# A memory-attention and squared-ReLU MLP kernel: all steps up to the last weight conversion issued in the order of a list schedule, batch 0 for 8 units, batch 1 for 16, then batch 0

## The chip, the cores and the metric

The kernel runs on one core of one Trainium2 chip. Its engines work side by side, each through its own queue in order: TensorE (PE, with PEld for weight loads), VectorE (DVE), ScalarE (ACT), GpSimd (POOL) and SyncE (SP), which issues the transfers. They wait for one another by semaphores. The metric is the device time of one execution in microseconds.

## The reference

Eight batches, 8 heads, 512 tokens of 64 numbers and 32 state rows per head. Tokens attend to the states and states to the tokens; the 544 rows per batch, 4,608 rows of 512 in all, go through an MLP with 2,048 hidden columns and a squared ReLU.

```python
scores = scale * np.matmul(x, state.transpose(0, 1, 3, 2))
a = softmax(scores)                      # over the 32 states
xread = np.matmul(a, state)
a2 = softmax(scale * np.matmul(state, x.transpose(0, 1, 3, 2)))   # over the 512 tokens
sread = np.matmul(a2, x)
x = concatenate([xread, sread])          # per batch, heads side by side
r = np.maximum(x @ w_in, 0.0)
return ((r * r) @ w_out).astype(np.float32)
```

The weights come as 64-bit floats, the inputs as 32-bit ones.

## The kernel before, in words

For tokens, x @ w_in is not formed from xread. Per batch the kernel computes z = state @ w_in (tile pz, line 151, then z_hi and z_lo) and multiplies it by the transposed attention a (a_hi, a_lo): ph = a z, line 314. Every 32-bit operand of the two big products is split into a rounded part hi (a cast by ScalarE, line 80) and a rest lo (a subtraction by VectorE, line 83), and hi·hi, lo·hi and hi·lo are added up.

The work is cut into units, one per batch and per f chunk of 128 hidden columns, 16 per batch. A unit has an up part, six products into ph (L314), relu on ScalarE (L316), a square (L318 on ScalarE for the first 16 units, L320 on VectorE after that), the split into g_hi and g_lo, and a down part two units later, twelve products into the four accumulators po (L340). z is made in pieces of one, two or four f chunks; z tiles of four chunks have two buffers, ph and g two, the raw weight tile three (RAW), the float tile wof one.

Before batch b's first unit its attention must stand: scores in pst (L196), a copy for the states' softmax (e, L208), a transposing move into q (L236), maximum, difference, exponential, sum, reciprocal and product (L243 to L252; L245 on ScalarE), a transposing move back into at (L255) and the split. Batch 0 does that in two halves, the others in one piece.

A weight pair covers two f chunks and 1 MB. wi_raw and wo_raw hold 64-bit words; a conversion is a scaling on ScalarE (L102) and a shift and two joins on VectorE (L105, L111, L115). w_in then lies in wi; w_out is made in wof and split into wo_hi and wo_lo. There are eight pairs of each.

Units come in the order of BOTH (line 61): batch 0 up to f chunk 4, batch 1 up to 8, batch 0 the rest, batch 1 the rest, then batches 2 to 7 and a last part for the states' rows. Each stretch ends with four moves or additions from po into sum. The first four units and what they need are written out by hand in begin (line 513), in a fixed order for VectorE, SyncE and ScalarE; keep holds back the lo subtraction of a step and issues it later. After that mlp (line 301) goes unit by unit, and aux issues, at two slots per unit, the conversions that are due (spread evenly by weights, line 575), z pieces and the later batches' attention; up to the end of batch 0 VectorE and SyncE keep the order of issue, with lo parts one slot late, while a scheduler places TensorE and ScalarE.

Of the kernel before, what the change touches and what calls it, by code (L numbers as in the profile page):

```python
# [9 lines left out]
F32 = mybir.dt.float32  # L10
# [8 lines left out]
def memory_attention_then_relu2_ffn(  # L19
# [41 lines left out]
    BOTH = ((0, 4), (1, 8), (0, NFC), (1, NFC))  # L61
    LATE = 2

# [4 lines left out]
    ps_x = ctx.enter_context(tc.tile_pool(name="ps_x", bufs=1, space=bass.MemoryType.PSUM))  # L68

# [7 lines left out]
    held = []  # L77

    def split(hi, lo, src, eng_lo):
        nc.scalar.copy(out=hi, in_=src)  # L80

        def rest():
            eng_lo.tensor_sub(out=lo, in0=src, in1=hi.bitcast(F32))  # L83

        held[-1].append(rest) if held else rest()

    def keep(step):

        held.append([])
        emit(step)  # L90
        parts_ = held.pop()
        return lambda: [f() for f in parts_]

    def singles(out_f, words):
# [7 lines left out]
        nc.scalar.activation(out_f, high.bitcast(F32), AF.Abs, scale=2.0**-112)  # L102
# [7 lines left out]
        def join():  # L110
# [3 lines left out]
            )  # L114
            mark[:] = [nc.vector.scalar_tensor_tensor(  # L115
# [4 lines left out]
        return shift, join  # L120
# [5 lines left out]
    def z_piece(b, units, first):  # L126

        def run():
            with tc.high_priority(offset=HURRY):
                make()  # L130

        def make():
# [23 lines left out]
            if not first:  # L156
                split(z_hi[:, :, dst], z_lo[:, :, dst], both[:, :, :width], nc.vector)
                return
            for g in range(NG):
                split(z_hi[:, g, dst], z_lo[:, g, dst], pz[g], nc.vector)  # L160
        return run
# [3 lines left out]
    def attention(b):  # L165
# [13 lines left out]
        def fetch_t():  # L179
            my["t"] = sb.tile([P, HG, S], F32, name="xt_raw", bufs=1)  # L180
# [10 lines left out]
        def scores():  # L191
# [16 lines left out]
            nc.scalar.copy(out=my["e2"], in_=pst)  # L208
# [17 lines left out]
        def soft(gs):  # L226
# [14 lines left out]
            def soft1():  # L241
                q1 = flat(my["q1"])
                nc.vector.tensor_reduce(out=flat(my["m1"])[:, :, 0], in_=q1, axis=AX.X, op=ALU.max)  # L243
                nc.vector.tensor_sub(out=q1, in0=q1, in1=wide(my["m1"]))
                nc.scalar.activation(q1, q1, AF.Exp, scale=SCALE)  # L245

            def soft1b():
                q1, s1 = flat(my["q1"]), flat(my["s1"])
                nc.vector.tensor_reduce(out=s1[:, :, 0], in_=q1, axis=AX.X, op=ALU.add)
                nc.vector.tensor_scalar_add(s1, s1, EPS)  # L250
                nc.vector.reciprocal(s1, s1)
# [49 lines left out]
    def mlp(parts, begin, aux):  # L301
# [45 lines left out]
        for n in range(begin(up, down), len(todo_) + 2):  # L347
# [8 lines left out]
            if n >= 2:  # L356
                down(n - 2)
# [361 lines left out]
```

## Time and profile before

| | us |
|---|---|
| median of 3 runs | 701.27 (701.07 to 701.54) |
| profiled execution | 701.49 |
| its span | 699.7 |
| PE busy | 660.0 |
| DVE busy | 374.5 |
| ACT busy | 290.4 |

The span runs from the first to the last instruction of the profiled execution. Of the chain that ended last, PE has 89%. The mean granted TensorE clock is 0.987. Busy time of PE has modelled ends, so a row of several products shows more than their start-to-start pace.

### The profile page before, as it was taken

What the parts mean: (1) busy time and instruction counts of PE and PEld (TensorE: products, weight loads), DVE (VectorE), ACT (ScalarE), POOL (GpSimd) and SP (SyncE); (2) the same over time, 40 slices, a digit from 0 to 9 for tenths busy, and PEclk for the clock granted to TensorE, in tenths of its full rate; (3) what the DMA queues carried; (4) which work ended last, traced back from release to release, by engine and by line L of the source; (5) the groups of instructions that cost most, each with busy time, mean ns of one, the idle gap of its engine ahead of it and who ended that gap; (6) DMA issues with size and microseconds to landing.
All of it is one profiled execution on the core that took longest, in us unless ns stands there. A gap on an engine that the chain in (4) does not pass through costs nothing.

```text
span 699.7 us, 9593 instructions
## 1 busy us (share of the span) xinstructions
PE 660.0 (94%) x3896; PEld 496.6 (71%) x3896; DVE 374.5 (54%) x528; ACT 290.4 (41%) x470; POOL 24.4 (3%) x44
## 2 busy tenths in 40 slices
PE   1675999999999999999999999999999999999996
PEld 0343777778777777678777776777768767788895
DVE  4868778864847534643356333743474334343553
ACT  3445576452534333433344233433343233333442
POOL 0000000000010100010001000100002000000000
PEclk9898899999999999999999999999999999999999
DMA  8333335203113001300040003100111001000101
GB/s 311 120 121 120 121 125 200 101 5 120 63 61 121 5 0 56 127 5 1 0 181 5 1 0 126 56 1 1 59 64 59 3 1 60 1 1 0 61 1 30
DMA packets 15803, 43.59 MB, mean 62 GB/s; under 512 B 1296, under 2 KB 3344, under 8 KB 13840
## 3 DMA queue, kind: packets, MB, share of 16 engines
q1 hardware_dynamic: 15568, 42.73, 17.1%
q8 instruction: 30, 0.49, 0.3%
q10 hardware_dynamic: 192, 0.26, 0.2%
q14 instruction: 13, 0.11, 0.0%
HBM read 34.08 MB, written 8.91 MB: 61 GB/s over the span
## 4 chain that ended last, share of the span: by engine, by line
PE 89%; DVE 2%; ACT 2%; issue 1%; DMA 1%; SPq 0%
PE po L340 53%; PE ph L314 28%; PE pz L151 4%; PE pst L196 1%; PE pr L279 1%; PE pt L267 1%; DMA wi_raw<-w_in 1%; DVE wof L115 0%; DVE wof L111 0%; ACT g_hi L80 0%; ACT wo_hi L80 0%; ACT z_hi L80 0%; ACT ph L318 0%; DVE wo_lo L83 0%; DVE wi L111 0%
## 5 line engine op out<-in xcount | busy, mean ns | idle before, releaser
L340 PE MATMUL po<-wo_hi,g_hi 128*128 128x512 f32 x544 | 216.9, 401 | 9.6 <-ACT wo_hi L80 4.9
L340 PE MATMUL po<-wo_lo,g_hi 128*128 128x512 f32 x544 | 214.7, 397 | 1.3 <-DVE wo_lo L83 1.2
L320 DVE TENSOR_TENSOR ph<-ph,r 128x512 f32<-128x512 f32 (+1 forms) x128 | 84.9, 663 | 134.2 <-ACT r L316 134.0
L316 ACT ACTIVATE r<-ph 128x512 f32<-128x512 f32 (+1 forms) x144 | 82.9, 575 | 177.5 <-PE ph L314 177.4
L340 PE MATMUL po<-wo_hi,g_lo 128*128 128x512 f32 x544 | 156.4, 394 | 0.0
L83 DVE TENSOR_TENSOR g_lo<-ph,g_hi 128x512 fp32r<-128x512 f32 (+1 forms) x144 | 94.7, 659 | 91.1 <-ACT g_hi L80 70.4
L340 PEld LDWEIGHTS po<-wo_hi,g_hi 128*128 128x128 f32 x544 | 103.0, 190 | 42.3 <-ACT g_hi L80 8.7
L80 ACT CAST g_hi<-ph 128x512 fp32r<-128x512 f32 (+1 forms) x144 | 81.1, 563 | 117.2 <-DVE ph L320 75.0
L340 PEld LDWEIGHTS po<-wo_lo,g_hi 128*128 128x128 f32 x544 | 103.0, 190 | 30.0 <-issue 6.7
L340 PEld LDWEIGHTS po<-wo_hi,g_lo 128*128 128x128 f32 x544 | 101.8, 189 | 22.4 <-issue 0.8
L314 PE MATMUL ph<-a_hi,z_hi 128*128 128x512 f32 x256 | 84.3, 412 | 7.9 <-ACT a_hi L80 5.8
L314 PE MATMUL ph<-a_hi,z_lo 128*128 128x512 f32 x256 | 82.8, 402 | 0.0
L314 PE MATMUL ph<-a_lo,z_hi 128*128 128x512 f32 x256 | 80.3, 396 | 0.0
L314 PEld LDWEIGHTS ph<-a_hi,z_hi 128*128 128x128 f32 x256 | 46.9, 192 | 32.6 <-ACT a_hi L80 8.2
L83 DVE TENSOR_TENSOR z_lo<-pz,z_hi 128x1024 fp32r<-128x1024 f32 (+2 forms) x39 | 40.0, 1029 | 41.6 <-ACT z_hi L80 41.5
L314 PEld LDWEIGHTS ph<-a_hi,z_lo 128*128 128x128 f32 x256 | 49.0, 192 | 16.1 <-issue 5.4
L314 PEld LDWEIGHTS ph<-a_lo,z_hi 128*128 128x128 f32 x256 | 48.4, 190 | 11.7 <-DVE wof L105 0.8
L80 ACT CAST z_hi<-pz 128x1024 fp32r<-128x1024 f32 (+2 forms) x39 | 33.3, 859 | 50.1 <-PE ph L314 26.7
L151 PE MATMUL pz<-wi,sp_raw 64*32 64x512 f32 (+2 forms) x592 | 36.9, 557 | 7.3 <-DVE wi L115 6.9
L290 POOL COPY sr<-rd 32x128 f32<-32x128 f32 x32 | 9.2, 288 | 393.0 <-DVE rd L284 391.9
L151 PEld LDWEIGHTS pz<-wi,sp_raw 64*32 64x32 f32 x592 | 6.8, 107 | 22.6 <-DVE wi L115 9.3
L196 PE MATMUL pst<-xt_raw,sp_raw 64*32 64x512 f32 x128 | 14.6, 714 | 8.1 <-DMA xt_raw<-xT 6.8
(61 smaller groups left out, 387.6 us busy)
## 6 DMA issues: line engine op xcount, KB each, us to landing
xt_raw<-xT SPq DMA_DIRECT2D x8, 1024.0 KB, 4.9
wo_raw<-w_out SPq DMA_DIRECT2D x8, 1024.0 KB, 4.9
xn_raw<-xn SPq DMA_DIRECT2D x8, 1024.0 KB, 5.7
out<-sum SPq DMA_DIRECT2D x32, 256.0 KB, 3.8
wi_raw<-w_in SPq DMA_DIRECT2D x7, 1024.0 KB, 4.8
wi_raw<-w_in SPq DMA_DIRECT2D x2, 512.0 KB, 6.9
sp_raw<-stP SPq DMA_DIRECT2D x8, 64.0 KB, 1.9
out<-os__5381 SPq DMA_DIRECT2D x2, 64.0 KB, 1.7
```

What stands on the lines that cost most here:

```text
L80: nc.scalar.copy(out=hi, in_=src)
L83: eng_lo.tensor_sub(out=lo, in0=src, in1=hi.bitcast(F32))
L151: nc.tensor.matmul(pz[g][j * N:(j + 1) * N], lhsT=state[b][rows, j, :], rhs=wi[rows, j, cols], start=True, stop=True,)
L196: nc.tensor.matmul(pst[j * N:(j + 1) * N, g, :], lhsT=state[b][rows, j, :], rhs=my["t"][rows, j, :], start=True, stop=True,)
L267: nc.tensor.transpose(out=pt[:, g, t, :], in_=my["e2"][:, g, t * P:(t + 1) * P], identity=ident)
L279: nc.tensor.matmul(pr[j * N:(j + 1) * N, g, :D], lhsT=my["e"][:, g, t, j * N:(j + 1) * N], rhs=my["n"][:, t, h * D:(h + 1) * D], start=t = ...
L290: nc.gpsimd.tensor_copy(out=sr[b // GB][at:at + N, j * NG * D:(j + 1) * NG * D], in_=rd[j * N:(j + 1) * N].rearrange("p g d -> p (g d)"),)
L314: nc.tensor.matmul(ph, lhsT=w, rhs=v, start=m == 0, stop=m == len(todo) - 1)
L316: nc.scalar.activation(r, ph, AF.Relu)
L320: nc.vector.tensor_mul(out=ph, in0=ph, in1=r)
L340: nc.tensor.matmul(po[t], lhsT=g, rhs=w, start=i == 0 and j == 0, stop=i == last and j == 2)
```

## The change

The hand-written begin and the spread of conversions give way to one plan over the first 24 units, those of the first two stretches, and everything they need. BOTH becomes batch 0 up to f chunk 8, batch 1 up to 16, batch 0 the rest; so there are three stretches in place of four. The helpers return their steps apart (parts_of gives the cast and the subtraction, singles gives scaling, shift and two joins, up gives five steps, the attention ten). Each step goes into Plan with an engine, an assumed duration, and the names of the steps it needs; buffers that must be free are written as needs too. run takes, again and again, the engine that can start first, and of its steps that can start within 0.35 of then the one with the longest chain behind it, and issues it; the assumed times only set the order. All four engines keep that order. Further: the copy of the scores (keep) comes after the transposing move, xT of batch 1 goes into the xn_raw buffer and is loaded before the first w_out, z pieces after the first stretch are always four chunks wide, and the loop after the plan places no conversions.

```diff
-    BOTH = ((0, 4), (1, 8), (0, NFC), (1, NFC))
+    BOTH = ((0, 8), (1, NFC), (0, NFC))
     LATE = 2
+    TURN = 4
...
+    class Plan:
+        def __init__(self):
+            self.steps, self.order = {}, []
+        def add(self, name, engine, cost, run, needs=(), more=0.0, line=None):
+            assert name not in self.steps
+            self.steps[name] = engine, cost, cost + more, run, set(needs) | {line} - {None}, line
+        def run(self):
+            users = {n: [] for n in self.steps}
+            for n, (*_, needs, _) in self.steps.items():
+                for m in needs:
+                    users[m].append(n)
+            rest, open_ = {}, {n: len(u) for n, u in users.items()}
+            todo = [n for n, u in open_.items() if not u]
+            while todo:
+                n = todo.pop()
+                _, _, took, _, needs, _ = self.steps[n]
+                rest[n] = took + max((rest[m] for m in users[n]), default=0)
+                for m in needs:
+                    open_[m] -= 1
+                    if not open_[m]:
+                        todo.append(m)
+            assert len(rest) == len(self.steps)
+            left = {n: len(needs) for n, (*_, needs, _) in self.steps.items()}
+            from_, free = dict.fromkeys(self.steps, 0.0), {}
+            ready = [n for n in self.steps if not left[n]]
+            while ready:
+                def first(engine):
+                    return max(free.get(engine, 0.0), min(
+                        from_[n] for n in ready if self.steps[n][0] == engine
+                    ))
+                now, _, engine = min(
+                    (first(e), str(e), e) for e in {self.steps[n][0] for n in ready}
+                )
+                n = max(
+                    (n for n in ready if self.steps[n][0] == engine and from_[n] <= now + NEAR),
+                    key=lambda n: rest[n],
+                )
+                ready.remove(n)
+                _, cost, took, run, _, _ = self.steps[n]
+                start = max(now, from_[n])
+                free[engine] = start + cost
+                run()
+                self.order.append((n, start))
+                for m in users[n]:
+                    to, *_, line = self.steps[m]
+                    done = start + (cost if line == n else took + (HOP if to != engine else 0))
+                    from_[m] = max(from_[m], done)
+                    left[m] -= 1
+                    if not left[m]:
+                        ready.append(m)
...
-    weights, reads = Ahead(), Ahead()
-    rest_ = [convert(kind, k) for k in range(2, NK) for kind in ("wi", "wo")][1:]
-    start, stop = 2 * ZC, 2 * (at[NFC - 2] - 2)
-    for n, s_ in enumerate(rest_):
-        now = start + n * (stop - start) // len(rest_)
-        weights.add([s_], now + 1, now)
+        planned = sum(len(fcs) for _, fcs in parts[:2])
+        plan = Plan()
+        add = plan.add
+        w0, w1, w2 = (attentions[b][1] for b in range(3))
+        loads = []
+        def load(name, mb, run, needs=()):
+            add(name, SP, 2.6 * mb, run, needs, 2.0, loads[-1] if loads else None)
+            loads.append(name)
+        load("state0", 0.5, lambda: emit(w0["pad"]))
+        load("xT0", 1.0, lambda: emit(w0["load_t"]))
+        load("wi0a", 0.5, lambda: load_w("wi", 0, (early,)))
+        load("wi0b", 0.5, lambda: load_w("wi", 0, (late,), raws["wi", 0]))
+        load("state1", 0.1, lambda: emit(w1["pad"]))
+        load("xT1", 1.0, lambda: emit(w1["load_t"]))
+        order_w = [("wi", 0)]
+        for k in range(NK):
+            order_w += [("wo", k)] if k else [("wo", 0), ("wi", 1)]
+            order_w += [("wi", k + 1)] if 0 < k < NK - 1 else []
+        for n, (kind, k) in enumerate(order_w[1:], 1):
+            load(
+                f"{kind}{k}", 1.0, lambda kind=kind, k=k: load_w(kind, k, (whole,)),
+                [f"{''.join(map(str, order_w[n - RAW]))}.join"] if n >= RAW else [],
+            )
+        load("state2", 0.1, lambda: emit(w2["pad"]))
+        def chain(b, needs):
+            _, w, softs = attentions[b]
+            width = S * NG // len(softs)
+            add(f"scores{b}", PE, 1.3, lambda: emit(w["scores"]), [f"xT{b}", *needs], 0.7)
+            turns = [f"turn{b}{h}" for h in range(len(softs))]
+            old = [f"low0{h}" for h in range(len(attentions[0][2]))] if b else []
+            for h, soft in enumerate(softs):
+                add(turns[h], DVE, dve(width), lambda s_=soft[0]: emit(s_), [f"scores{b}", *old], HOP)
+            add(f"keep{b}", ACT, act(NG * S), lambda: emit(w["keep"]), turns, HOP)
+            for h, soft in enumerate(softs):
+                before = f"turn{b}{h}"
+                for name, engine, cost, step in zip(
+                    ("top", "less", "exps", "total", "inverse", "norm", "back", "high", "low"),
+                    (DVE, DVE, ACT, DVE, DVE, DVE, DVE, ACT, DVE),
+                    (dve(width),) * 2 + (act(width), dve(width), 0.4) + (dve(width),) * 2
+                    + (act(width), dve(width)),
+                    soft[1:],
+                ):
+                    add(f"{name}{b}{h}", engine, cost, lambda s_=step: emit(s_), [before], HOP)
+                    before = f"{name}{b}{h}"
+            return [f"{name}{b}{h}" for name in ("high", "low") for h in range(len(softs))]
...
+        a_ready = {0: chain(0, ["state0"])}
+        px = ["keep0"]
+        z_ready, chunks = {}, []
+        while pieces and pieces[0][0] < planned + 3:
+            first, b, cover = pieces.pop(0)
+            if len(z_ready) == TURN:
+                a_ready[1] = chain(1, ["state1"] + px)
+                px = ["keep1"]
+            chunk = b, cover[0] // ZC
+            if chunk not in chunks:
+                chunks.append(chunk)
+            needs = [f"scores{b}"] + [have[fc] for fc in cover]
+            if len(chunks) > 2:
+                ob, oc = chunks[-3]
+                needs += [f"up{ob}.{fc}" for fc in range(oc * ZC, (oc + 1) * ZC)]
+            alone = first < 2
+            product, high, low = z_piece(b, cover, alone)
+            name, width = f"z{b}.{cover[0]}.", len(cover) * NG * P
+            if not alone:
+                needs += px
+                px = [name + "high", name + "low"]
+            add(name + "up", PE, 0.5 + 0.6 * width / 1024, product, needs, 0.4)
+            add(name + "high", ACT, act(width), high, [name + "up"], HOP)
+            add(name + "low", DVE, dve(width), low, [name + "high"], HOP)
+            z_ready.update({(b, fc): [name + "high", name + "low"] for fc in cover})
+        units = [f"{b}.{fc}" for b, fcs in parts for fc in fcs]
+        firsts = {sum(len(fcs) for _, fcs in parts[:n]) for n in range(1, len(parts))}
+        line = None
+        for n in range(planned):
+            u = units[n]
+            b, fc = map(int, u.split("."))
+            product, relu, square, high, low = up(n)
+            add(
+                f"up{u}", PE, 6 * MM, product,
+                z_ready[b, fc] + a_ready[b] + ([f"low{units[n - 2]}"] if n >= 2 else []),
+                0.25, line,
+            )
+            line = f"up{u}"
+            add(
+                f"relu{u}", ACT, act(S), relu,
+                [line] + ([f"square{units[n - 1]}"] if n else []), HOP,
+            )
+            on = (ACT, act(S)) if n < NFC else (DVE, dve(S))
+            add(f"square{u}", *on, square, [f"relu{u}"], HOP)
+            add(
+                f"high{u}", ACT, act(S), high,
+                [f"square{u}"] + ([f"end{units[n - 2]}"] if n >= 2 and n - 2 < planned - 2 else []),
+                HOP,
+            )
+            add(f"low{u}", DVE, dve(S), low, [f"high{u}"], HOP)
+            if n < 2:
+                continue
+            u = units[n - 2]
+            fc = int(u.split(".")[1])
+            steps = down(n - 2)
+            needs = [f"high{u}", f"wo{fc // 2}.high", f"wo{fc // 2}.low"]
+            if n == 2:
+                needs += ["z0.0.low", "z0.1.low"]
+            if n - 2 in firsts:
+                needs += rows
+            add(f"down{u}", PE, 8 * MM, steps[0], needs, 0.2, line)
+            add(f"end{u}", PE, 4 * MM, steps[1], [f"low{u}"], 0.25, f"down{u}")
+            line = f"end{u}"
+            rows = []
+            for t, step in enumerate(steps[2:]):
+                rows.append(f"row{u}.{t}")
+                add(rows[-1], *((ACT, act(S)) if t % 2 else (DVE, dve(S))), step, [line], HOP)
+        with tc.manual_schedule(engines={PE, DVE, ACT, SP}):
+            plan.run()
+        slot[0] = 2 * planned
+        return planned
```

convert, left out here, adds scale on ScalarE and shift, sign and join on VectorE, for w_out also high and low; each needs the one before and the first needs the load. A w_out pair's scale also needs the low of the pair before. The attention of batch 1 enters the plan after four units' z (TURN), behind their use of the shared accumulator.

What that does to the queue of VectorE, at three places. The first is what stands ahead of the z_lo of unit 0 (written from pz_137 before, from pz_145 now), near the program's start. L249 to L252 are the sums and products of batch 0's first softmax half (now L264 to L275), L278 is the transposing move back. Before:

```order
L111 SCALAR_TENSOR_TENSOR wi<-wi_raw,wi 128x4x128
L115 SCALAR_TENSOR_TENSOR wi<-wi_raw,wi 128x4x128
L249 TENSOR_REDUCE s_112<-q_110 128x16
L250 TENSOR_SCALAR s_112<-s_112 128x16
L251 RECIPROCAL s_112<-s_112 128x16
L252 TENSOR_TENSOR q_110<-q_110,s_112 128x512
L83 TENSOR_TENSOR z_lo<-pz_137,z_hi 128x128
L83 TENSOR_TENSOR z_lo<-pz_138,z_hi 128x128
```

Now:

```order
L120 SCALAR_TENSOR_TENSOR wi<-wi_raw,wi 128x4x128 x2
L275 TENSOR_TENSOR q_100<-q_100,s_102 128x512 x2
L278 STREAM_TRANSPOSE at<-q_100 128x512 x2
L108 TENSOR_SCALAR wi<-wi 128x4x256
L108 TENSOR_SCALAR wof<-wof 128x1024
L114 SCALAR_TENSOR_TENSOR wi<-wi_raw,wi 128x4x256
L87 TENSOR_TENSOR a_lo<-at,a_hi 128x512 x2
L87 TENSOR_TENSOR z_lo<-pz_145,z_hi 128x128
L87 TENSOR_TENSOR z_lo<-pz_146,z_hi 128x128
```

The z_lo rows moved behind both softmax halves, the move back, both half-pair conversions, the first shifts of w_in 1 and w_out 0, and a_lo.

The second place is around the end of w_out pair 0 (wo_lo), where the first g_lo stand. wof is the single float buffer. Before:

```order
L115 SCALAR_TENSOR_TENSOR wof<-wo_raw,wof 128x1024
L236 STREAM_TRANSPOSE q_226<-pst 128x1024
L83 TENSOR_TENSOR wo_lo<-wof,wo_hi 128x1024
L83 TENSOR_TENSOR g_lo<-ph,g_hi 128x512 x2
L105 TENSOR_SCALAR wi<-wi 128x4x256
L111 SCALAR_TENSOR_TENSOR wi<-wi_raw,wi 128x4x256
L115 SCALAR_TENSOR_TENSOR wi<-wi_raw,wi 128x4x256
L105 TENSOR_SCALAR wof<-wof 128x1024
```

Now:

```order
L87 TENSOR_TENSOR z_lo<-pz,z_hi 128x2x256
L87 TENSOR_TENSOR wo_lo<-wof,wo_hi 128x1024
L108 TENSOR_SCALAR wof<-wof 128x1024
L114 SCALAR_TENSOR_TENSOR wof<-wo_raw,wof 128x1024
L108 TENSOR_SCALAR wi<-wi 128x4x256
L87 TENSOR_TENSOR g_lo<-ph,g_hi 128x512
```

The shift of the next w_out pair moved from behind the w_in conversion to directly behind wo_lo, and the transposing move of batch 1 left this place.

The third place is the maximum of batch 1's softmax (m_227 before, m_263 now) and what follows it. Before:

```order
L115 SCALAR_TENSOR_TENSOR wof<-wo_raw,wof 128x1024
L243 TENSOR_REDUCE m_227<-q_226 128x32
L244 TENSOR_TENSOR q_226<-q_226,m_227 128x1024
L83 TENSOR_TENSOR wo_lo<-wof,wo_hi 128x1024
L83 TENSOR_TENSOR g_lo<-ph,g_hi 128x512 x2
L249 TENSOR_REDUCE s_228<-q_226 128x32
L250 TENSOR_SCALAR s_228<-s_228 128x32
L251 RECIPROCAL s_228<-s_228 128x32
L252 TENSOR_TENSOR q_226<-q_226,s_228 128x1024
L83 TENSOR_TENSOR z_lo<-pz,z_hi 128x1024
L255 STREAM_TRANSPOSE at<-q_226 128x1024
```

Now (the difference is L257, the conversion rows L108 to L120):

```order
L245 STREAM_TRANSPOSE q_262<-pst 128x1024
L120 SCALAR_TENSOR_TENSOR wi<-wi_raw,wi 128x4x256
L120 SCALAR_TENSOR_TENSOR wof<-wo_raw,wof 128x1024
L87 TENSOR_TENSOR g_lo<-ph,g_hi 128x512 x2
L87 TENSOR_TENSOR z_lo<-pz,z_hi 128x2x256
L251 TENSOR_REDUCE m_263<-q_262 128x32
L87 TENSOR_TENSOR wo_lo<-wof,wo_hi 128x1024
L257 TENSOR_TENSOR q_262<-q_262,m_263 128x1024
L108 TENSOR_SCALAR wi<-wi 128x4x256
L114 SCALAR_TENSOR_TENSOR wi<-wi_raw,wi 128x4x256
L108 TENSOR_SCALAR wof<-wof 128x1024
```

The steps of the softmax stand one at a time between conversion rows of w_in and w_out and g_lo rows, where before they stood in runs with the g_lo of two units as a pair ahead of the sum.

More of the change, by code (lines that the diff above doesn't have):

```diff
@@ L114, in join @@
             )
+        def join():
             mark[:] = [nc.vector.scalar_tensor_tensor(
@@ L118, in join @@
             )]
-        return shift, join
+        return scale, shift, sign, join
     mark = []
@@ L126, in z_piece, with product @@
     def z_piece(b, units, first):
[L128 to L132, printed above, removed]
+        my = []
+        def product():
             c, at = divmod(units[0], ZC)
@@ L155, in make @@
             z_hi, z_lo = zt[b, c]
[L156 to L161, printed above, removed]
+            if first:
+                my.extend(
+                    parts_of(z_hi[:, g, dst], z_lo[:, g, dst], pz[g], nc.vector) for g in range(NG)
+                )
+            else:
+                my.append(parts_of(z_hi[:, :, dst], z_lo[:, :, dst], both[:, :, :width], nc.vector))
+        return product, lambda: [h() for h, l in my], lambda: [l() for h, l in my]
     state = {}
@@ L295, in attention @@
         steps = dict(
-            pad=pad, load_t=load_t, scores=scores, exps2=exps2, load_n=load_n, turn=turn, read=read
+            pad=pad, load_t=load_t, scores=scores, keep=keep, exps2=exps2, load_n=load_n, turn=turn,
+            read=read,
         )
-        return pair, steps, [soft(gs) for gs in halves]
+        return pair, steps, [soft(gs) if b < 2 else grouped(*soft(gs)) for gs in halves]
     def mlp(parts, begin, aux):
@@ L462, in memory_attention_then_relu2_ffn @@
     whole, early, late = slice(0, 2 * P), slice(0, P), slice(P, 2 * P)
-    queue = [(kind, k) for k in range(NK) for kind in ("wi", "wo")]
-    loaded, ready = [0], set()
-    def load_next():
-        if loaded[0] < len(queue):
-            n = loaded[0]
-            load_w(*queue[n], (whole,) if n else (early, late))
-            loaded[0] += 1
-    def convert(kind, k, u=whole):
-        def run():
-            for step in started(kind, k, u):
-                step()
-        return run
-    def started(kind, k, u=whole):
-        shift, join, parts_ = convert_w(kind, k, u)
-        def finish():
-            join()
-            parts_()
-            if kind == "wi":
-                ready.update(range(2 * k + u.start // P, 2 * k + u.stop // P))
-            if u.stop == 2 * P:
-                load_next()
-        return shift, finish
@@ L571, in next_z @@
[L571 to L580 removed]
+        while pieces and slot[0] >= 2 * (pieces[0][0] - 3):
+            _, b, cover = pieces.pop(0)
+            with tc.high_priority(offset=HURRY):
+                for step in z_piece(b, cover, False):
+                    step()
@@ L591, in aux @@
     def aux():
-        if slot[0] >= 2 * ends[0]:
-            for f in pending:
-                f()
-            pending.clear()
-            fixed.close()
-            ahead()
-        else:
-            old = pending[:]
-            pending.clear()
-            for f in old:
-                f()
-            pending.append(keep(ahead))
+        ahead()
         slot[0] += 1
     def ahead():
-        weights.run()
         z_due()
```

288 lines of the change are left out of this document (150 added, 138 removed).

## The prediction, made before the changed kernel ran

> **What bounds the kernel now.** I read the table of stretches first, then the waits of TensorE and of VectorE, then the rows at the points where stages begin. In the table each row is a stretch of the span, its length, the busy time and count of PE, PEld, DVE, ACT and POOL, the granted TensorE clock, the DMA share and GB/s.
>
> ```profile
> 0.00:8.84 8.84, 1.96 (x16) 0.26 (x16) 0.00 (x0) 1.28 (x1) 0.70 (x6) 1.00 0.77 257
> 8.84:20.00 11.16, 2.64 (x32) 0.48 (x32) 9.77 (x20) 5.92 (x9) 0.00 (x0) 1.00 0.71 284
> 20.00:30.00 10.00, 6.15 (x29) 3.81 (x30) 7.30 (x12) 6.50 (x12) 0.00 (x0) 0.96 0.42 126
> 30.00:40.00 10.00, 8.64 (x40) 5.80 (x39) 7.21 (x8) 1.76 (x3) 0.00 (x0) 0.70 0.34 123
> 40.00:50.00 10.00, 7.35 (x40) 4.37 (x40) 7.22 (x7) 5.21 (x8) 0.00 (x0) 1.00 0.45 172
> 50.00:60.00 10.00, 4.08 (x17) 2.85 (x16) 7.82 (x10) 6.61 (x9) 0.00 (x0) 1.00 0.00 1
> 60.00:70.00 10.00, 6.86 (x32) 4.11 (x31) 7.70 (x8) 5.00 (x8) 0.00 (x0) 0.67 0.60 210
> 70.00:81.42 11.42, 11.42 (x57) 8.66 (x55) 7.60 (x11) 6.24 (x9) 0.00 (x0) 0.84 0.29 94
> 100.00:120.00 20.00, 18.61 (x93) 14.31 (x93) 17.26 (x22) 13.12 (x20) 0.00 (x0) 1.00 0.43 146
> 120.00:162.66 42.66, 42.66 (x234) 32.02 (x233) 30.59 (x44) 19.80 (x35) 0.00 (x0) 1.00 0.17 67
> ```
>
> From 120 us on TensorE never pauses; nothing that reorders the start can shorten that part. Everything to be won lies before: between 8.84 and 81.42 us neither TensorE nor VectorE is full. Who waits there:
>
> ```profile
> PE pz L151 <- DVE wi L115: 6.9, 1, 6.9
> PE pst L196 <- DMA xt_raw<-xT: 6.8, 1, 6.8
> PE ph L314 <- ACT a_hi L80: 5.8, 2, 4.4
> PE po L340 <- ACT wo_hi L80: 4.9, 2, 2.9
> PE po L340 <- ACT g_hi L80: 4.7, 2, 3.1
> ```
>
> ```profile
> DVE q L236 <- ACT e L208: 12.7, 2, 9.9
> DVE g_lo L83 <- ACT g_hi L80: 9.0, 3, 3.7
> DVE z_lo L83 <- ACT z_hi L80: 3.1, 2, 2.7
> DVE wo_lo L83 <- ACT wo_hi L80: 0.8, 1, 0.8
> DVE s L249 <- ACT q L245: 0.3, 1, 0.3
> ```
>
> TensorE waits for attention and weights that VectorE and ScalarE make; VectorE in turn stands behind single operands of ScalarE with other work queued after them. Up to 81.42 us its waits are 12.7 + 9.0 + 3.1 + 0.8 + 0.3 = 25.9 us. The first 9.9 is the start; **16.0 us** are holes that another order could fill.
>
> I measure by two points that both kernels have. One unit (batch, f chunk) is six products into ph, so point A, the first product of the ninth unit, is where 48 rows of L314 lie behind; point B is the first turn of a batch (L267), with 26 units begun and 24 units' down products done in both orders.
>
> ```profile
> 81.42 0.62 PE L314 MATMUL ph<-a_hi,z_hi 128*128 128x512 f32 x2
> 83.71 0.39 PE L340 MATMUL po<-wo_hi,g_hi 128*128 128x512 f32 x1
> 162.66 1.04 PE L267 MATMUL pt<-ident,e 128*128 128x128 f32 x8
> ...
> 81.42:162.66 81.24, 5.92 (x112) 1.27 (x112) 1.00 0.30 107
> ```
>
> A is at 81.42, B at 162.66; ten products go from 81.42 to 83.71, so one takes 0.229 us at full clock. The last row is the z products (L151) alone between A and B.
>
> **The change, term by term.** After B both programs hold the same units in the same order with the z pieces shifted by a few products, so I let the stretch from B to the end cost what it cost, and sum two gains.
>
> *Up to A.* Before the ninth unit the new VectorE order holds this, and all of it must be done, since that unit needs the z_lo of batch 1's first chunk, the 60th row of that queue: both softmaxes, w_in pairs 0 to 3, w_out pairs 0 to 2, the arithmetic of pair 3, z_lo, six g_lo. That is almost what the old queue did by 81.42: the DVE column adds up to 9.77 + 7.30 + 7.21 + 7.22 + 7.82 + 7.70 + 7.60 = **54.6 us**. The differences, from the groups of VectorE in that stretch:
>
> ```profile
> L115 DVE SCALAR_TENSOR_TENSOR wof<-wo_raw,wof 128x1024 int32<-128x1024 int32 x4 | 4.9, 1225 | 0.1
> L83 DVE TENSOR_TENSOR g_lo<-ph,g_hi 128x512 fp32r<-128x512 f32 x7 | 4.7, 686 | 9.0 <-ACT g_hi L80 9.0
> L83 DVE TENSOR_TENSOR z_lo<-pz,z_hi 128x512 fp32r<-128x512 f32 x2 | 1.4, 687 | 2.7 <-ACT z_hi L80 2.7
> L365 DVE COPY sum<-po 128x512 f32<-128x512 f32 x2 | 1.3, 681 | 0.0
> ```
>
> The fourth w_out join, only begun at 81.42, is whole now: +1.1. No sum is copied yet: -1.3. One g_lo fewer, -0.7; one narrow z_lo more, +0.7. So 54.4, and 0.9 us that lay between instructions beyond the named waits (81.42 - 25.9 - 54.6): 55.3.
>
> The queue starts earlier. The first transposes stood behind a copy of the same scores by ScalarE; now they come first:
>
> ```profile
> 6.79 1.96 PE L196 MATMUL pst<-xt_raw,sp_raw 64*32 64x512 f32 x16 [6.79 <-DMA xt_raw<-xT]
> 8.84 1.01 ACT L208 COPY e<-pst 128x1024 f32<-128x1024 f32 x1 [6.82 <-PE pst L196]
> 9.89 1.31 DVE L236 STREAM_TRANSPOSE q<-pst 128x512 f32<-128x512 f32 x2 [9.89 <-ACT e L208]
> ```
>
> So VectorE begins at 8.8, 1.1 earlier.
>
> What holes stay? I followed the new queues row by row with these durations and find three.
>
> ```profile
> 22.16 1.05 PE L314 MATMUL ph<-a_hi,z_lo 128*128 128x512 f32 x2
> L102 ACT ACTIVATE wof<-wo_raw 128x1024 f32<-128x1024 f32 x3 | 3.4, 1143 | 2.5 <-issue 2.5
> L316 ACT ACTIVATE r<-ph 128x512 f32<-128x512 f32 x4 | 2.4, 599 | 4.1 <-PE ph L314 4.1
> ```
>
> First, unit 0: its z_lo is now the 18th row and comes at 24.3 instead of the 20.97 at which the old first unit starts. Six products at the slow pace seen here (0.43 each) end at 26.9, and relu, square and cast at 0.60 end at 28.8; VectorE has emptied what stands ahead of that g_lo at 28.2: 0.6 us. Second, w_out's float buffer wof is single: the row after wo_lo is a shift that needs the next scaling, which needs the buffer: 1.2 us, with g_lo and the second softmax queued behind. Third, w_in pair 3 was loaded after pair 1's buffer came free, and its scaling comes late: about 0.9. With crumbs I take **3.1 us**. Bounds: 1.2, the buffer alone; and 8, half of the old 16.0, if the in-order waits come out as badly as half by hand.
>
> Loads cost nothing: xT of batch 1 moves ahead of w_out 0 and w_in 1, but the same bytes lie in the first burst, which ends before 17 us (0 GB/s from 17 on):
>
> ```profile
> 16.00:17.00 1.00, 0.34 (x16) 0.00 (x0) 0.90 (x4) 0.67 (x4) 0.00 (x0) 1.00 0.48 197
> 17.00:18.00 1.00, 0.35 (x8) 0.26 (x16) 1.00 (x4) 0.90 (x1) 0.00 (x0) 1.00 0.00 0
> ```
>
> The last load now is w_in 1; scaled (1.14) by 18.2, its shift comes up in the queue at 20.3. That 2.1 us is the cover; a landing later than this adds to the holes one for one.
>
> So batch 1's first z_lo ends at 8.8 + 55.3 + 3.1 = 67.2; the z product of its second chunk goes before the ninth unit, 512 of the 2,560 columns that took 5.92 us in the L151 row above, 1.2 us: A at **68.4**, a gain of 13.0.
>
> *From A to B.* The old stretch takes 81.24. It holds 1.39 idle (20.00 - 18.61), a g_lo behind a w_out conversion; the new queue has g_lo where its g_hi ends: -1.4. Seven z pieces (four of 256 columns, three of 512, 5.92 us) become four of 512: 2,048 of 2,560 columns, -1.2. Against that I set one stretch of half clock after the pause before A (1.7 us idle, so perhaps 1 us) and 0.5 us where unit 20 waits for its z_lo: +1.5. VectorE's own work up to unit 20 is 42 us (four weight pairs' 3.1 + 4.3 us less one w_out, thirteen g_lo, four squares, two z_lo, two copies; at 1.225 an operation of full width a w_in pair is 2.5 of them, a w_out pair 3.5), 67.2 + 42 = 109, and TensorE gets there at 68.4 + 12 x 4.1 + 2 = 120: 11 us of cover. So 80.1, a gain of 1.1; B at **148.5**.
>
> Sum: 13.0 + 1.1 = 14.1 us. The profiled execution took 701.49 (span 699.7 and 1.8 around it), 0.22 over the median of 701.27. Against the median: 701.3 - 14.1 = **687.2 us**.
>
> **The rivals.** *Holes return (smaller gain).* A list that assumes durations fixes four queues; where one is wrong, an instruction at the head holds all behind it. For it: the old hand order lost 16.0 us so. Against: the waits it lost them to are named, and the new order stands two or three ready instructions before each g_lo. With 8 us of holes A is at 73.3; with two more half-clock stretches of 1.7 each the gain is 14.1 - 4.9 - 3.4 = 5.8: 695.5.
>
> *The clock stays at half (slower).* The new TensorE order is busy in short bursts from 24.3 to 68.4. The old record lost clock after three pauses there (0.96, 0.70, 0.67, 0.84). Work in that stretch: 48 + 72 products at 0.229 = 27.5, z pieces about 5, scores 2, so 34 of 44 us. All at half clock it takes 68 and A comes at 92.3, 10.9 later than before: 701.3 + 10.9 - 1.1 = 711.1. It decides against the change once two thirds of that work, 23 of 34, run at half clock. Against it: two of the old drops stand at pauses of 2.88 and 4.39 us (the rows at 29.71 and 59.20; in the first, four products take 2.08); the new pauses that I find are under 2, and TensorE's share rises from 73% (44.5 of 61.4) to 77%.
>
> ```profile
> 20.00:81.42 61.42, 44.50 (x209) 29.60 (x209) 44.85 (x54) 31.33 (x46) 0.00 (x0) 0.86 0.35 120
> 29.71 2.08 PE L340 MATMUL po<-wo_hi,g_hi 128*128 128x512 f32 x4 [2.88 <-ACT wo_hi L80]
> 59.20 0.72 PE L314 MATMUL ph<-a_hi,z_hi 128*128 128x512 f32 x2 [4.39 <-ACT a_hi L80]
> ```
>
> The Trainium skill, "TensorE: Matmul & The Clock Gate", section "HAM oscillation — how this bites in real kernels", says that frequent micro-idles between groups of matmuls make the clock swing between half and full, which speaks for this rival; its table in Part 1 asks for an idle window of about 3.4 us before the clock drops, which speaks against it. The 2.88 us pause above, with a drop, agrees with neither to the letter.
>
> **How the numbers follow.** The forecast (gain 10 to 18): 0.70. Holes return (gain 10 down to none): 0.24, of which 0.03 lies within 0.2% of no change, about what a measurement of this kernel can tell. Half clock: 0.06. So faster 0.91, same 0.03, slower 0.06. Range: with 1.2 us of holes and no half clock after A the gain is 14.1 + 1.9 + 1.0 = 17.0, so 684.3; I go to 683.0 for a shorter start. Above, 695.5 from the first rival.
>
> **What would show it.** Right: ninth unit at 68 (65 to 74), first turn near 148, VectorE over 90% busy between 9 and 67, waits of VectorE there about 3 us, same length from B on. Wrong: VectorE idle over 8 us before A; a clock under 0.8 between 30 and 66; B earlier while the end is not, which would mean that the common part was not common.

## The result, and the profile after

The changed kernel takes **684.25 us** (median of 4 runs, 683.95 to 684.99), against 701.40 (701.07 to 701.81) for the kernel before beside it: ratio 0.9757, 95% interval 0.974 to 0.9774. The gain is 17.1 us where 14.1 was forecast, and the time lies inside the range of 683.0 to 695.5.

The profiled execution took 684.99 with a span of 682.82. The table of stretches for the kernel after follows (stretch, length, then busy time and count of PE, PEld, DVE, ACT, POOL, granted clock, DMA share, GB/s); the last three rows are from the queue's start to the end of batch 1's first z_lo, from A to B, and from B to the end.

```profile
8.64:20.00 11.36, 1.54 (x33) 0.73 (x33) 11.29 (x23) 6.78 (x12) 0.00 (x0) 1.00 0.82 312
20.00:30.00 10.00, 7.25 (x29) 4.15 (x30) 9.81 (x15) 3.54 (x7) 0.00 (x0) 1.00 0.45 170
30.00:40.00 10.00, 10.00 (x51) 7.17 (x51) 7.73 (x10) 7.58 (x12) 0.00 (x0) 1.00 0.31 113
40.00:50.00 10.00, 8.44 (x49) 5.67 (x48) 9.40 (x11) 7.59 (x11) 0.00 (x0) 1.00 0.50 204
50.00:60.00 10.00, 9.90 (x66) 6.13 (x65) 9.90 (x13) 7.12 (x11) 0.00 (x0) 1.00 0.56 212
...
8.64:64.13 55.49, 39.66 (x232) 25.57 (x232) 52.22 (x72) 36.24 (x53) 0.00 (x0) 1.00 0.51 195
65.21:145.80 80.59, 79.48 (x397) 61.24 (x389) 56.51 (x71) 44.23 (x68) 0.00 (x0) 1.00 0.27 98
145.80:682.82 537.02, 531.06 (x3213) 406.48 (x3211) 258.99 (x380) 207.31 (x346) 23.64 (x38) 1.00 0.12 41
```

VectorE is now busy in 52.22 of 55.49 us (94%) before A. The same stretch from B to the end of the kernel before, and the whole of both kernels up to B:

```profile
162.66:699.71 537.05, 531.03 (x3213) 406.50 (x3211) 258.21 (x379) 205.70 (x342) 23.66 (x38) 1.00 0.12 41
...
0.00:162.66 162.66, 128.96 (x684) 90.13 (x685) 116.31 (x151) 84.67 (x129) 0.70 (x6) 0.95 0.37 132
```

```profile
0.00:145.80 145.80, 122.13 (x653) 87.25 (x653) 109.82 (x143) 82.42 (x123) 0.70 (x6) 1.00 0.40 147
```

The rest is common to 0.03 us (537.05 and 537.02): all 16.9 us lie before B. Of them TensorE's pauses give 33.70 - 23.67 = 10.0, and its busy time 128.96 - 122.13 = 6.8. Most of the 6.8 is rate: the products into po are 288 up to B in both kernels and take 76.03 us before and 71.24 after, since the old order ran part of them in its stretches at half clock (0.96, 0.70, 0.67 and 0.84 in the prediction's table). The fewer and wider z products give 0.5 (10.79 and 10.25 us). The points, in the timeline of the kernel after:

```profile
64.18 1.09 PE L154 MATMUL pz<-wi,sp_raw 64*32 64x512 f32 x16 [1.65 <-DVE z_lo L87]
65.21 0.73 PE L362 MATMUL ph<-a_hi,z_hi 128*128 128x512 f32 x2
...
145.80 1.03 PE L311 MATMUL pt<-ident,e 128*128 128x128 f32 x8
```

A came from 81.42 to 65.21 and B from 162.66 to 145.80. B is the better mark, because A does not stand behind the same work in both. These rows count the products into po up to A (busy PE and count, busy PEld and count), before and then after:

```profile
0.00:81.42 81.42, 24.37 (x80) 17.21 (x80) 0.90 0.44 158
```

```profile
0.00:65.21 65.21, 18.51 (x72) 13.27 (x72) 1.00 0.55 207
```

The old order issues eight products of unit 6 ahead of the ninth unit, the new one behind it. At the prediction's 0.229 us each these are 1.8 us, so of A's 16.2 us about 1.8 only moved behind A.

What VectorE still waits for up to 66 us:

```profile
DVE q L245 <- PE pst L203: 8.6, 1, 8.6
DVE wof L108 <- ACT wof L105: 2.2, 1, 2.2
DVE z_lo L87 <- ACT z_hi L84: 0.5, 1, 0.5
```

The first is the start. The 16.0 us of holes have become 2.7.

### The profile page after: what moved, and what is told of

Its sections match the earlier page's. It is cut to its first block, busy times and chain, and to the rows that moved or that the text cites. A ratio compares the mean times of both kernels' runs of the same rounds, so it can differ in the third digit from the quotient of the medians.

```text
span 682.8 us, 9542 instructions
## 1 busy us (share of the span) xinstructions
PE 653.2 (96%) x3864; PEld 493.7 (72%) x3864; DVE 368.8 (54%) x522; ACT 289.7 (42%) x468; POOL 24.3 (4%) x44
## 4 chain that ended last, share of the span: by engine, by line
PE 90%; DVE 6%; issue 1%; ACT 1%; DMA 1%; SPq 0%; DVEq 0%; ACTq 0%
PE po L405 53%; PE ph L362 28%; PE pz L154 4%; PE pst L203 2%; PE pr L323 1%; PE pt L311 1%; DMA xt_raw<-xT 1%; DVE wof L114 1%; DVE wo_lo L87 1%; DVE z_lo L87 1%; DVE wi L114 1%; DVE wi L120 1%; DVE a_lo L87 0%; DVE q L275 0%; DVE m L251 0%
## 5 line engine op out<-in xcount | busy, mean ns | idle before, releaser
L405 PE MATMUL po<-wo_hi,g_lo 128*128 128x512 f32 x544 | 154.3, 393 | 0.0
L405 PEld LDWEIGHTS po<-wo_hi,g_lo 128*128 128x128 f32 x544 | 100.7, 188 | 24.8 <-issue 3.8
```

The costliest lines, as they stand in the source:

```text
L405: nc.tensor.matmul(po[t], lhsT=g, rhs=w, start=i == 0 and j == 0, stop=i == last and j == 2)
```

## The experiments

Each run is the changed kernel with one edit, or with two of these edits together, executed four times unless it says once. Dots mark code left out. Each also makes the sum tiles on first use (`if b not in sums` for `if t == 0`), which moves no instruction by itself. A and B are the two points of the prediction.

### The batches in their old order

```diff
-    BOTH = ((0, 8), (1, NFC), (0, NFC))
+    BOTH = ((0, 4), (1, 8), (0, NFC), (1, NFC))
-        planned = sum(len(fcs) for _, fcs in parts[:2])
+        planned = sum(len(fcs) for _, fcs in parts[:3])
```

> The changed kernel with the old stretches (batch 0 for 4 units, batch 1 for 8, batch 0 for 12), still 24 units in the plan and still the list's order. Theory, that the order of steps carries the gain by filling VectorE's holes: the softmax of batch 1 is due four units earlier, two weight pairs of each kind four units later, so unit 4 starts near 47 us instead of 41.9, unit 8 near 66 instead of 65.2, and the time is 684.5 to 687. Rival, that the new sequence of batches carries it: half of the 17 us or more is given back, 692 or more.

685.01 us (683.61 to 685.22), ratio 0.9759 [0.9745, 0.9774]: the same as the whole change. A lies at 65.68, B at 146.01, though VectorE's holes are others:

```profile
DVE q L245 <- PE pst L203: 8.8, 1, 8.8
DVE wo_lo L87 <- ACT wo_hi L84: 2.5, 1, 2.5
DVE s L264 <- ACT q L261: 0.8, 1, 0.8
DVE g_lo L87 <- PE po L405: 0.6, 1, 0.6
DVE wi L108 <- ACT wi L105: 0.6, 1, 0.6
DVE z_lo L87 <- ACT z_hi L84: 0.6, 1, 0.6
DVE g_lo L87 <- ACT g_hi L84: 0.3, 1, 0.3
```

Without the start 5.4 us of holes are left. The new order of the batches carries none of the gain that these runs can see. What is left is the plan, with the order of steps that it finds. The wider z pieces, which are part of it, were not taken back in a run of their own; the 0.5 us of TensorE above is all that is known of them.

### The list with another priority

```diff
-                    key=lambda n: rest[n],
+                    key=lambda n: -place[n],   # place: first added, first taken
```

> The changed kernel with the same plan, but among the steps that can start the first one added is taken instead of the one with the longest chain behind it. VectorE then does nearly all conversions before the sums of batch 0's softmax, some 60 us. Theory, that the priority carries the gain: unit 0 near 75 us, the first turn near 187, 720 to 730 in all. Rival, that issuing when ready is what counts: 684 to 695.

737.11 us (executed once), 36 us above the kernel before. TensorE's longest wait up to 78 us:

```profile
PE ph L362 <- ACT a_hi L84: 52.2, 1, 52.2
```

and the costliest groups of VectorE from 8 to 76 us begin with

```profile
L114 DVE SCALAR_TENSOR_TENSOR wi<-wi_raw,wi 128x1024 int32<-128x1024 int32 (+1 forms) x9 | 10.0, 1106 | 0.3
...
L87 DVE TENSOR_TENSOR wo_lo<-wof,wo_hi 128x1024 fp32r<-128x1024 f32 x8 | 9.7, 1210 | 0.0
```

All eight w_out pairs and eight w_in pairs are converted first and the first unit begins at 76.71. The engines, tiles and needs are the same, so issuing a step when it can start is not enough. The gain hangs on which of the ready steps is taken, and a poor choice costs more than the 16.0 us of holes in the hand order. The size was missed.

### The copy of the scores first

```diff
+            add(f"keep{b}", ACT, act(NG * S), lambda: emit(w["keep"]), [f"scores{b}"], HOP)
...
-                add(turns[h], DVE, dve(width), lambda s_=soft[0]: emit(s_), [f"scores{b}", *old], HOP)
-            add(f"keep{b}", ACT, act(NG * S), lambda: emit(w["keep"]), turns, HOP)
+                add(turns[h], DVE, dve(width), lambda s_=soft[0]: emit(s_), [f"keep{b}", *old], HOP)
...
```

> The changed kernel with ScalarE's copy of the scores ahead of VectorE's transposing move, as before the change. By the prediction's term the queue of VectorE starts 1.1 us later and everything up to the ninth unit with it: 685.4. Rival: VectorE only needs something to do, the list puts the first half-pair's shift and first join (0.4 + 0.7 us) in front of the move, and the time stays at 684.0 to 684.7.

684.5 us (683.32 to 685.17), ratio 0.9754 [0.974, 0.9769]; A 64.92. Nothing is lost. The start of VectorE's queue shows why:

```profile
8.50 0.43 DVE L108 TENSOR_SCALAR wi<-wi 128x512 int32<-128x512 int32 x1 [8.50 <-ACT wi L105]
8.96 0.69 DVE L114 SCALAR_TENSOR_TENSOR wi<-wi_raw,wi 128x512 int32<-128x512 int32 x1
9.57 1.31 DVE L245 STREAM_TRANSPOSE q<-pst 128x512 f32<-128x512 f32 x2
```

The list puts a weight conversion into the gap. The prediction's "starts 1.1 us earlier" was real as a time, but it was no gain of its own: any work ready by then fills it.

### A second buffer for w_out's float tile

```diff
-        wf = sb.tile([P, 2, DM], F32, name="wof", bufs=1)
+        wf = sb.tile([P, 2, DM], F32, name="wof", tag="xt_raw" if k % 2 else "wof", bufs=1)
-            wait = [f"wo{k - 1}.low"] if kind == "wo" and k else []
+            wait = [f"wo{k - 2}.low"] if kind == "wo" and k > 1 else []
```

> The changed kernel with a second float buffer for w_out pairs, in the place of the first xT tile, so that the scaling of pair 1 no longer waits for the subtraction of pair 0. Theory, that VectorE sets the start of the ninth unit: its 2.2 us hole at 30 us closes, unit 8 starts near 63, the time is 682 to 682.7. Rival, that TensorE at half clock up to 32 us sets it: the hole moves to another wait, 684 to 685.

**680.36 us** (680.23 to 680.87), ratio 0.9699 [0.9683, 0.9715]: better than both kernels. VectorE's waits up to 66 us:

```profile
DVE q L245 <- PE pst L203: 8.6, 1, 8.6
DVE g_lo L87 <- ACT g_hi L84: 0.2, 1, 0.2
```

A is at 62.26, 2.95 us earlier, for holes of 2.2 and 0.5 that are gone: VectorE's idle time up to A is time that TensorE loses, as the prediction's sum has it. A further 1.35 us comes from A to B (79.23 against 80.59), where unit 20 waits for nothing now.

### Shift and joins as one step of the plan

```diff
-            add(name + "shift", DVE, dve(width, 1), step(1), [name + "scale"], HOP)
-            add(name + "sign", DVE, dve(width), step(2), [name + "shift"], HOP)
-            add(name + "join", DVE, dve(width), step(3), [name + "sign"], HOP)
+            add(
+                name + "join", DVE, dve(width, 1) + 2 * dve(width),
+                lambda: [steps[i]() for i in (1, 2, 3)], [name + "scale"], HOP,
+            )
```

> The changed kernel with shift and both joins of a conversion as one step of the plan, so that they stand next to each other on VectorE as before the change. Theory, that a VectorE instruction right behind the one whose result it reads starts about 0.12 us later than behind an independent one, and that this is why the work up to the ninth unit took 52.7 us where 55.3 were predicted: 7 whole and 2 half conversions with two such neighbours each give back 1.7 to 2.2 us, 686 to 686.6. Rival, that the 2.6 us came from somewhere else: 684 to 685, with steps of equal length in both orders.

684.93 us (684.4 to 685.18), ratio 0.9761 [0.9747, 0.9776]; A 65.25, B 145.30. The time did not move, yet the run does not tell the theories apart: the conversions took 24.8 us up to A instead of 23.4, as the theory of the neighbours wants, but another order took away the hole at w_out's buffer, two others opened (1.7 us for a g_hi and 1.0 for batch 1's scores, 2.7 again), and one w_out subtraction fell behind A. So it was run again with the hole closed in both, against the run with two buffers:

> Second buffer for w_out's float tile, and shift and both joins of a conversion as one step of the plan. In the joined run with one buffer VectorE's work grew by 1.4 us and its small gaps by 0.5, but another order closed the hole at the buffer and the time did not move. Theory: neighbours of one conversion on VectorE, each reading the other's result, step 1.25 us apart instead of 1.14, and with the hole gone in both this shows: up to A about 14 such steps, 14 x 0.11 = 1.5 and 0.4 of gaps, A at 64.1 instead of 62.26, 682.3 us. Rival: it is the order of the list and not the neighbours that sets the time, and 680.4 stays within 0.5 us.

686.26 us (686.08 to 686.73), ratio 0.9785 [0.9769, 0.9801], 5.9 us worse than 680.36 where 1.9 were expected. A came at 64.23, as the theory had it (64.1): VectorE's 73 instructions that begin before A, the same in both, take 1.3 us more and the small gaps between them 0.5 more. But B is at 147.32, 5.8 late. TensorE's busy time up to B is the same (120.1 and 120.2 us), so all of it is pauses: 3.8 us more up to the first unit and 2.1 more after A. A marks only the products of up; a z product that stood before A in the other run now stands behind it, so A alone showed too little. TensorE's timeline where the first unit begins:

```profile
24.64 1.22 PE L362 MATMUL ph<-a_hi,z_hi 128*128 128x512 f32 x2
```

It starts 5.0 us later than with steps apart (19.67): in one piece, conversions stand ahead of batch 0's attention that were taken apart around it. So joining the steps makes VectorE slower, and makes the list coarser; how the 5.9 us divide between the two stays open. The run with one buffer starts its first unit as late (24.46) and pauses 3.6 us more up to there than the changed kernel, but it wins this back: 1.5 us of pauses between the first unit and A, 1.0 after A, and 1.7 of busy time up to B (122.13 and 120.46). Why two buffers joined win nothing back was not tested.

### More products before the first unit

```diff
+        def warm():                       # 24 products of 64x512 into a spare ph tile
+            ...
+        add("warm", PE, 7.0, warm, ["scores0"], 0.0)
```

> The changed kernel with 24 extra products of TensorE (64 x 512, results unused) between the scores of batch 0 and the first z product, where TensorE waits 8.1 us, so that its clock is at full rate from about 15 us instead of 32.2. Theory, that VectorE's queue sets the ninth unit: the 18 products of units 0 to 2 get faster, but all that it brings is an earlier relu of unit 1 and so a shorter hole at 30 us (2.2 to 1.2): 683.0 to 684.2. Rival, that half clock up to 32 us costs what it slows: 18 x 0.2 us and half a microsecond of z, 680 to 680.6.

684.19 us (683.89 to 684.6), ratio 0.9754 [0.9738, 0.977]; A 64.42. No change, as the theory has it. The test was weaker than meant, though, as the products after the extra ones show:

```profile
27.85 1.05 PE L365 MATMUL ph<-a_hi,z_lo 128*128 128x512 f32 x2
28.70 1.05 PE L365 MATMUL ph<-a_lo,z_hi 128*128 128x512 f32 x2
29.55 0.69 PE L365 MATMUL ph<-a_hi,z_hi 128*128 128x512 f32 x2
```

They still run at half rate (28.70 - 27.85 for two, 0.43 each) up to 29.55, and the run with other loads, without extra products, had full rate from 29.0. What full rate from the first unit on would be worth is therefore not tried; that it would be little follows only from VectorE being full there.

### The loads of batch 1 later

```diff
-        load("xT1", 1.0, lambda: emit(w1["load_t"]))
+            if n == 2:      # in the loop over weights: after w_out 0 and w_in 1
+                load("xT1", 1.0, lambda: emit(w1["load_t"]))
```

> The changed kernel with xT of batch 1 loaded after the first w_out and the second w_in, as before the change; the two weight loads land about 2.6 us earlier. Theory, that no row of VectorE waits for these landings: unit 8 at 65.2, 684.0 to 684.8. Rival, that they do through ScalarE, which waited 1.3 us for w_in 1 with the casts of z behind it: 1 us less, 683.3.

684.43 us (683.85 to 684.95), ratio 0.9757 [0.9742, 0.9771]; A is 1.1 earlier, at 64.12, but the median does not show it. The loads cost nothing that the medians can tell.

### w_out's lo part on GpSimd

```diff
-            wo[0][:, 2 * k:2 * k + 2, :], wo[1][:, 2 * k:2 * k + 2, :], wf, nc.vector
+            wo[0][:, 2 * k:2 * k + 2, :], wo[1][:, 2 * k:2 * k + 2, :], wf, nc.gpsimd
...
-                add(name + "low", DVE, dve(width), step(5), [name + "high"], HOP)
+                add(name + "low", POOL, 2.5, step(5), [name + "high"], HOP)
...
-        with tc.manual_schedule(engines={PE, DVE, ACT, SP}):
+        with tc.manual_schedule(engines={PE, DVE, ACT, SP, POOL}):
```

> The changed kernel with the lo subtraction of w_out pairs on GpSimd, where one of this size takes 2.4 us (L83 for the later batches' a_lo). Theory, that VectorE's sum sets the ninth unit: four subtractions of 1.14 us leave its queue ahead of it, 1.2 us come back because the single float buffer is held longer: unit 8 near 62, 680.5 to 682. Rival, that the buffer chain or the two engines at once slow the rest as much: 684 or more.

683.11 us (682.52 to 683.47), ratio 0.9737 [0.9723, 0.9752]: between the two. A is at 64.36. VectorE loses four subtractions of 1.14 but its holes grow to 3.9 us, and three of its instructions take 0.6, 0.8 and 1.3 us longer than elsewhere. TensorE also pauses for 1.71 us up to 41.70 and for 0.62 up to 43.06, and then goes at half clock, as the granted clock of this stretch shows (third number from the end):

```profile
43.43:46.84 3.41, 3.41 (x10) 2.67 (x9) 3.23 (x4) 3.17 (x4) 0.18 (x1) 0.50 0.75 288
```

To see whether the one buffer or the other engine ate the gain, both edits together:

> Second buffer for w_out's float tile and w_out's lo subtraction on GpSimd, together. Where each stands: the second buffer alone 680.36 us with A (first product of the ninth unit) at 62.26 and no holes in VectorE; the subtraction on GpSimd alone 683.11 with A at 64.36 and 3.9 us of holes. Theory: VectorE's own work sets A once the holes are gone. Four subtractions of 1.14 leave it (-4.5), and some of its instructions that start while GpSimd works are held until GpSimd ends (three in the run with GpSimd alone, 0.55 + 0.81 + 1.29 = 2.6 us more than usual), so A comes at 62.3 - 4.5 + 2.6 = 60.4 and the time is 678.5; up to 675.9 if none is held. Rival: the later release of the tile (2.4 us on GpSimd against 1.2 on VectorE) or ScalarE is the limit, not VectorE's work: holes of 2 us or more come back and the time is 680.4 or more.

689.93 us (689.38 to 690.19), ratio 0.9836 [0.9821, 0.9851]: far worse than either alone, and neither theory. VectorE has no holes up to A, yet A is at 64.75: its own instructions swelled. GpSimd's timeline of this run, then VectorE's:

```profile
49.21 3.30 POOL L88 TENSOR_TENSOR wo_lo<-wof,wo_hi 128x1024 fp32r<-128x1024 f32 x1 [11.04 <-ACT wo_hi L85]
...
61.29 2.69 POOL L88 TENSOR_TENSOR wo_lo<-wof,wo_hi 128x1024 fp32r<-128x1024 f32 x1 [8.78 <-ACT wo_hi L85]
```

```profile
35.82 1.24 DVE L246 STREAM_TRANSPOSE q<-pst 128x1024 f32<-128x1024 f32 x1
36.99 2.27 DVE L121 SCALAR_TENSOR_TENSOR wi<-wi_raw,wi 128x1024 int32<-128x1024 int32 x1
...
50.30 3.29 DVE L115 SCALAR_TENSOR_TENSOR wof<-wo_raw,wof 128x1024 int32<-128x1024 int32 x1
...
61.63 2.90 DVE L109 TENSOR_SCALAR wi<-wi 128x1024 int32<-128x1024 int32 x1
```

A join of 1.22 us that begins inside GpSimd's 49.21 to 52.51 ends at 53.59, 1.08 after it; a shift of 0.68 inside 61.29 to 63.98 ends at 64.53, 0.55 after it. So they look held until GpSimd's end. The transposing move at 35.82, which reads the accumulator memory (pst), ran at its usual 1.24 beside GpSimd's second subtraction (35.20 to 38.17), and the join at 36.99 did not: it ended at 39.26, 1.09 after that one.

The Trainium skill, "SBUF — State Buffer", section "SBUF: two separate sides", has this as a rule: VectorE and GpSimd share one pair of ports by an exclusive lock for a whole instruction, against VectorE's fast one-input forms and those with two inputs from that memory (SBUF, where the tiles other than pst, pz, ph and po lie), and whichever starts first has them. The trace agrees, the numbers above beside it; I had set 2.6 us for it. GpSimd is held as well: its subtraction took 2.37 to 2.40 us up to A in the run with GpSimd alone and takes 2.55 to 3.30 here, and a shift at 49.58, just ahead of the join at 50.30, ran through it in its usual 0.68.

Up to A four of VectorE's instructions are held and take 2.58, 2.27, 3.29 and 2.90 us, 11.0 in place of 4.3. So the lock cost 6.7, more than the 4.6 that the four subtractions would have taken. From A to B the run takes 86.6 us where two buffers alone take 79.2: 4.4 of pauses and 3.0 of busy time. There one such hold (3.32 us) stands ahead of a unit's z_lo, and TensorE waits 4.05 us and goes on at half rate (two products here in 1.01, 0.46 at full rate):

```profile
105.46 1.22 PE L363 MATMUL ph<-a_hi,z_lo 128*128 128x512 f32 x2 [4.05 <-DVE z_lo L88]
```

With one buffer only three of VectorE's instructions were held before A, for 2.6 us, which fits the smaller harm of the edit alone. The plan knew nothing of the lock: it only had 2.5 us for the step.

## Why the prediction was right, point by point

**What bounds the start.** Right. VectorE is 94% busy from 8.64 to 64.13 (over 90% was asked for), and closing its last holes moves A and B by at least as much (680.36 us with two buffers).

**A, forecast 68.4, measured 65.21.** The end of batch 1's first z_lo was set at 8.8 + 55.3 + 3.1 = 67.2 and is 64.13. By terms:

- *Start*: 8.64 for 8.8. Right in size, but no gain of its own (the run with the copy first).
- *VectorE's own work*: **the mis-sized term**. 54.4 was set and 52.22 measured, with 0.5 for 0.9 of small gaps. I took over the old DVE column and changed only which steps it holds; but the old order had the two joins of a conversion next to each other, the new one puts other work between. VectorE's timeline of the kernel before, and then of the kernel after:

```profile
70.12 1.22 DVE L111 SCALAR_TENSOR_TENSOR wi<-wi_raw,wi 128x1024 int32<-128x1024 int32 x1
71.37 1.23 DVE L115 SCALAR_TENSOR_TENSOR wi<-wi_raw,wi 128x1024 int32<-128x1024 int32 x1
72.52 0.68 DVE L83 TENSOR_TENSOR g_lo<-ph,g_hi 128x512 fp32r<-128x512 f32 x1
```

```profile
33.01 1.23 DVE L114 SCALAR_TENSOR_TENSOR wof<-wo_raw,wof 128x1024 int32<-128x1024 int32 x1
34.15 0.69 DVE L108 TENSOR_SCALAR wi<-wi 128x1024 int32<-128x1024 int32 x1
```

Before, from a join to the one that reads its result 1.25 us, and 1.15 to the next that doesn't; after, 1.14. With each row counted up to the start of the next, conversions up to A took 25.0 us before and 23.4 after, 1.6 less, and the attention's 27 steps 18.5 and 17.5, 1.0 less; small differences in the other rows put 0.4 back, which leaves the 2.2.

- *Holes*: 3.1 forecast, 2.7 measured, right in the sum and wrong in the parts. Unit 0's g_lo (0.6) and w_in 3's scaling (0.9) found other work; the float buffer's hole was 2.24 for 1.2. ScalarE's timeline shows what I left out:

```profile
29.95 0.60 ACT L367 ACTIVATE r<-ph 128x512 f32<-128x512 f32 x1 [1.17 <-PE ph L362]
30.58 0.60 ACT L373 ACTIVATE ph<-r 128x512 f32<-128x512 f32 x1
31.12 1.12 ACT L105 ACTIVATE wof<-wo_raw 128x1024 f32<-128x1024 f32 x1
```

wo_lo frees the buffer at 30.04, but relu and square of a unit that ends late stand ahead of the scaling in ScalarE's order.

- *Loads*: nothing, right (the run with other loads).
- *z product before A*: 1.2 forecast, 1.08 from z_lo's end to A.

Together the terms make up the 3.2 us by which A came early, 2.6 of it from VectorE's own work and small gaps. That the gain of 17.1 meets the prediction's best case of 17.0 is luck: that case took holes of 1.2 us, and they were 2.7.

**From A to B, forecast 80.1, measured 80.59.** Right within 0.5, but by luck, because wrong parts cancel. The eight products into po that the old order had done before A (80 against 72, above) now lie in this stretch, 1.8 us that the sum left out. The z products fell by 1.5 (5.92 to 4.42 us) for 1.2. The half-clock stretch of 1.0 did not come: the PEclk column is 1.00 throughout, and no pause between 32 and 146 us is longer than 1.7. Unit 20's wait was set at 0.5 and is 1.11, with this queue of VectorE:

```profile
113.56 2.33 DVE L225 TENSOR_REDUCE nm<-e 128x2 f32<-128x1024 f32 x2
115.81 0.69 DVE L375 TENSOR_TENSOR ph<-ph,r 128x512 f32<-128x512 f32 x1
116.41 1.22 DVE L87 TENSOR_TENSOR wo_lo<-wof,wo_hi 128x1024 fp32r<-128x1024 f32 x1
117.54 0.23 DVE L226 TENSOR_SCALAR nm<-nm 128x2 f32<-128x2 f32 x2
117.68 1.22 DVE L87 TENSOR_TENSOR z_lo<-pz,z_hi 128x1024 fp32r<-128x1024 f32 x1
```

The 11 us of cover that I gave VectorE's work do not help here: what delays z_lo is an order, two maxima (L225) of the second softmax and a w_out subtraction ahead of it, not an amount. The gain from A to B is thus 0.65 for 1.1: the 1.39 us pause of the old order gave way to one of 1.11, and TensorE's busy time fell by only 0.4 (79.85 to 79.48). The clock cost nothing.

**After B.** Common to 0.03 us, as assumed.

**The rivals.** *Holes return*: no, 2.7 us is less than a fifth of the old 16.0. The mechanism is real, though, and unpriced cases of it cost much (737.11 with another priority, 689.93 with GpSimd). *The clock stays at half*: no. TensorE ran at half rate up to 32.2 us (two products of up take 0.85 from start to start at 28.01 and 28.86; the clock column does not show it there) and kept the full rate from then until the last 2 us; the Trainium skill's swing of the clock between groups of products ("TensorE: Matmul & The Clock Gate", section "A second HAM failure mode: psum-queue depth-cycling", not the section that the prediction names) is not seen here, where the longest pause is 1.7 us. But other runs show the clock fall. In the run with GpSimd alone two pauses close together, 1.71 and 0.62 us, were followed by 3.41 us at half clock; in the run with GpSimd and two buffers a pause of 2.24 us and one of 4.05 us were each followed by as much, and in the run with the old stretches one of 3.80. The kernel before, on the other hand, kept the full clock over a pause of 1.97 us up to 46.85. So the length of one pause does not tell whether the clock drops; what does was not tested.

## What to carry to other kernels

Where one engine's queue sets the start, add up its own work and its named waits, not those of the engine that waits: sum and holes forecast the new time within 3 us. Check that two marks stand behind the same work before you subtract them. Put work that does not depend on its neighbour between dependent VectorE instructions, and look for single buffers whose release stands behind another engine's order; one more buffer was worth another 3.9 us here. A step moved to GpSimd is not free for VectorE: count which of VectorE's instructions will start under it.

## What was not expected of the hardware

- A 128x1024 VectorE instruction is followed after 1.14 us by one that doesn't read its result, after 1.25 by one that does.
- A GpSimd subtraction of 128x1024 takes 2.4 to 3.4 us, and VectorE's joins and shifts that start within it are mostly held to its end (2.27 and 3.29 us for 1.22, 2.90 for 0.68), while instructions that read pst, pz or ph run on (1.24, 0.69 and 0.68 us). One shift of 0.68 was not held; there GpSimd's subtraction is the longer one (3.30).
- Two pauses of TensorE of 1.71 and 0.62 us close together were followed by 3.41 us at half clock (0.50 from 43.43 to 46.84 in the run with GpSimd alone).
- 24 extra products of 64x512 from 8 us on did not bring TensorE to its full rate earlier than about 29 us, which a run without them reached as well.
